# One recurrence-and-experts kernel: the token rows written in another order, by GpSimd's DMA queue in place of ScalarE's

## The chip, the cores and the metric

The kernel runs on one core of a Trainium2 chip. A core has TensorE (PE in the profile; its weight loads PEld), VectorE (DVE), ScalarE (ACT), GpSimd (POOL) and SyncE (SP), each with its own in-order instruction queue, and 16 DMA engines that all queues share. SP, ACT and POOL can start DMAs. A matrix product goes from SBUF to PSUM; what leaves PSUM is copied by VectorE or ScalarE.

The metric is the device time of one execution in microseconds. The kernel before takes 568.6 us, the median of three runs from 563.7 to 569.66.

## The reference

Two parts, one after the other. The first is a recurrence over 768 steps for 4 batches and 8 heads, with a state of 40 x 40 for each:

```python
for t in range(S):
    y[:, :, t] = np.einsum('bhd,bhde->bhe', rt, state)
    Sa = np.einsum('bhde,bhe->bhd', state, at)
    state_decay = state * wt[:, :, None, :] - np.einsum('bhd,bhe->bhde', Sa, bt)
    state = state_decay + np.einsum('bhd,bhe->bhde', vt, kt)
```

Its output y is turned into x, with 3072 rows (one a token, number batch * 768 + t) of 320 values. The second part picks one of 8 experts for each row, keeps for each expert the 80 rows with the largest gate value, and leaves all other rows of the output zero:

```python
expert_idx = np.argmax(x @ w_gate, axis=1)
tok_idx = ...            # the expert's rows, at most `capacity` of them, by gate_w
h = np.maximum(x[tok_idx] @ w1[e], 0.0)
out[tok_idx] = gate_w[tok_idx, None] * (h @ w2[e])
```

## The kernel before

**Tiling.** The sequence is cut into chunks of T = 64 steps (NCI = 12 chunks), and the batches into NP = 2 pairs. A unit is a chunk of a pair: 24 units, n = 2 * chunk + pair, and each fills 128 partitions with 2 batches x 64 steps. Four units make a batch of units (`batches`, six of them, kq = 0 to 5 in the code; the text says batch 0 to 5). For a chunk the recurrence is a triangular system. `prepare` makes decays and score matrices of a unit, `finish` makes its output and the new state, `gate` the gate values of a group of units. Groups are the same as batches, but for the last four units, which form two groups of two.

**The triangular systems.** Batch 0 is inverted by products on PE (`doubling`). For batches 1 to 5 `invert` writes the 32 x 32 diagonal blocks to HBM (L657, SP), reads them back with one block to a partition (`fetch`, L661, POOL), and eliminates on POOL: 30 steps of a multiply (L677) and an add (L679), a mask, a memset, and a copy that turns the blocks (`flip`, L691). POOL then writes both forms to HBM (`put`, L697: `solved`, `flipped`). SP brings them back into the layout of the units: d<-flipped (L719), nt<-solved (L713), d<-solved (L706). `solve` builds the rest of the inverse from these with two products, the first at L737 and the second at L752; ACT copies between them (gt, L742).

**Rows and gates.** ACT copies a unit's x into `xg` (L992), which holds one group. VectorE makes the gates (L1020 to L1034), and puts the gate value in the row's last column (L1033). `ids_go` (L1039, POOL) multiplies the one-hot expert choice with two numbers for each token, the tile `tok`. `rows_go` (L1048) writes `xg` to `x_rows` in HBM, in the order batch * 768 + t, by one DMA of 160.5 KB for each batch parity and pair of units, on ACT's queue. Eight DMAs on ACT's queue (L1118) write zeros over the output, 480 KB each.

**What sets the order.** A planner (`Plan`) takes every step with an engine, a planned duration, a lag, a due time and what it reads and writes, and lists all steps in one order. The calls are made in that order, so each engine's queue holds its steps in the list's order. `add("ACT", ...)` names the engine for the plan alone; the call inside the step decides which queue gets the instruction. The list around the fifth group, with planned times, reads: ... 357.24 flip of batch 5 (POOL), 358.36 `xg` of group 4 (VectorE), 358.66 `rows_go` of group 4 (ACT), 359.39 and 360.39 the two puts of batch 5 (POOL), 361.39 `ids_go` of group 4 (POOL). The eight zero steps stand at planned times 67, 102, 136, 166, 197, 224, 255 and 280.

**The second part.** After the last gate VectorE finds each expert's limit, PE turns the one-hot places into row numbers, and VectorE makes from them idx_g (which rows of x_rows to gather, L1224) and idx_s (which rows of the output to write, L1233). POOL gathers 128 rows at a time (L1155); six passes through the experts' two layers follow, and POOL scatters the results (L1303).

Of the kernel before, what the change touches and what calls it, by code (L numbers as in the profile page):

```python
# [8 lines left out]
F32 = mybir.dt.float32  # L9
# [4 lines left out]
Alu = mybir.AluOpType  # L14
# [3 lines left out]
class Plan:  # L18
# [7 lines left out]
    def add(self, eng, us, lag, when, fn, reads=(), writes=(), psum=None, to=()):  # L26
        whole = eng == "PE" and psum[0][0] in WHOLE
        o = dict(eng=eng, us=us, lag=lag, when=when, stage=self.stage, fn=fn, whole=whole, i=len(self.ops), deps=set(), psum=None,
                 reads=list(reads), writes=list(writes), to=list(to))
        if psum:  # L30
            key, n = psum
            if key not in self.width:
                self.width[key] = n
                o["psum"] = key
            o["writes"].append(key)
        o["kind"] = f"{eng} {(psum[0] if psum else [*o['writes'], *o['reads'], ('none', 0)][0])[0]}"
        for key in o["reads"]:
            for p, wrote in self.touch.get(key, ()):
                if wrote:
                    o["deps"].add(p)  # L40
        for key in o["writes"]:
            for p, _ in self.touch.get(key, ()):
                o["deps"].add(p)
        for key in o["reads"]:
            self.touch.setdefault(key, []).append((o["i"], False))
        for key in o["writes"]:
            self.touch.setdefault(key, []).append((o["i"], True))
        self.ops.append(o)
# [140 lines left out]
def kernel(  # L189
# [19 lines left out]
    nc = tc.nc  # L209
    B, H, S, D = r.shape  # L210
    N, DM = out.shape
    E = moe_w_gate.shape[1]
    F = moe_w1.shape[2]
    cap = min(int(moe_capacity), N)
    T, C, HB = 64, 32, 64
    NCI = S // T
    NP = B // 2
# [85 lines left out]
    with ExitStack() as p1:  # L303
# [88 lines left out]
        def iotas():  # L392
            nc.gpsimd.iota(first_i, pattern=[[-1, E]], base=E, channel_multiplier=0)
            for bb in range(2):
                nc.gpsimd.iota(tok_i[T * bb : T * bb + T, 0:NCI], pattern=[[1, NCI], [2 * NCI, NP]],
                               base=1 + NCI * bb, channel_multiplier=0)
                nc.gpsimd.iota(tok_i[T * bb : T * bb + T, NCI], pattern=[[0, NP]], base=0, channel_multiplier=1)

        add("POOL", 1.5, 0.1, -600.0, iotas, (), [("iotas", 0)])
# [601 lines left out]
        def gate(gi):  # L1001
# [40 lines left out]
            add("POOL", 0.8, 0.1, z + 1, ids_go, [sm, ("gates", gi), ("late", 0)], [("ids", gi), *([("og", gi)] if nu == GU else [])])  # L1042

            def rows_go():
                dst = x_dram[:, :].rearrange("(p b c t) d -> b t c p d", p=NP, b=2, t=T)
                for bb in range(2):
                    for i in range(nu // NP):
                        nc.scalar.dma_start(dst[bb, :, ns[0] // NP + i],  # L1048
                                          xg[T * bb : T * bb + T, NP * i : NP * i + NP, :])
            add("ACT", 0.65 * nu, 2.0, z + 2, rows_go, [("xg", gi)], ())  # L1050

            def ranks(src, dst, keys, us, wide):
# [62 lines left out]
                [("early", e), ("nt", NM + e), *((k_, NM + 2 * e + i) for i in range(2) for k_ in SLOT)])  # L1115
        zrows = 384
        for i in range(N // zrows):
            add("ACT", 0.7, 2.0, 0.0, lambda i=i: nc.scalar.dma_start(  # L1118
                out[i * zrows : (i + 1) * zrows, :].rearrange("(p r) (h d) -> p (r h) d", p=128, h=2),
                zero.to_broadcast([128, zrows // 64, DM // 2])), [("W", 2 * i)])  # L1120

# [31 lines left out]
    def gather(p):  # L1153
        rows[p] = fs.tile([128, XW], F32, name="rows", tag="rows", bufs=NPASS)
        nc.gpsimd.indirect_dma_start(  # L1155
            out=rows[p][:, 0:XW], out_offset=None, in_=x_dram[:, :],
            in_offset=bass.IndirectOffsetOnAxis(ap=of_pass(idx_g, p), axis=0))
# [6 lines left out]
    with ExitStack() as p2:  # L1164
        sl = p2.enter_context(tc.tile_pool(name="sl", bufs=1))
        ps_l = p2.enter_context(tc.tile_pool(name="ps_l", bufs=1, space=PSUM))
        NSEL = E * 2 * NM
        at = sl.tile([128, NM, 2 * E], F32, name="at")
        idle = ps_l.tile([128, NSEL], F32, name="idle")

        def keep_warm(n):
            for _ in range(n):
                nc.tensor.matmul(idle, lhsT=ident, rhs=at.rearrange("p m a -> p (m a)"), start=True, stop=True)

        thr = sl.tile([E, 1], F32, name="thr")
        nc.vector.tensor_scalar_max(thr, best[:, cap - 1 : cap], 1e-6)
        thw = sl.tile([E, 128], F32, name="thw")
        nc.vector.tensor_copy(thw, thr.to_broadcast([E, 128]))
        thp = ps_l.tile([128, E], F32, name="thr_p")
        nc.tensor.transpose(thp, thw, ident[:E, :E])  # L1180
        tb = sl.tile([128, E, 1], F32, name="tb")
        nc.vector.tensor_copy(tb[:, :, 0], thp)
        sel = sl.tile([128, E, 2, NM], BF16, name="sel")
        for i, op in enumerate((Alu.is_gt, Alu.is_equal)):
            nc.vector.tensor_tensor(out=sel[:, :, i, :], in0=gates.rearrange("p m e -> p e m"),
                                    in1=tb.to_broadcast([128, E, NM]), op=op)
        selm = sel.rearrange("p e i m -> p (e i m)")
        pos = ps_l.tile([128, NSEL], F32, name="pos")
        nc.tensor.matmul(pos, lhsT=less_b, rhs=selm, start=True, stop=False)
        upto = sl.tile([128, NSEL], BF16, name="upto")  # L1190
        nc.vector.tensor_tensor_scan(upto, seg.rearrange("p e m -> p (e m)"), selm, 0.0, op0=Alu.mult, op1=Alu.add)
        nc.tensor.matmul(pos, lhsT=ones_b, rhs=upto, start=False, stop=True)
        nc.vector.scalar_tensor_tensor(out=at.rearrange("p m a -> p a m"), in0=pos.rearrange("p (a m) -> p a m", m=NM), scalar=1.0,
                                       in1=sel.rearrange("p e i m -> p (e i) m"), op0=Alu.add, op1=Alu.mult)
        slot = sl.tile([128, NM, 1], F32, name="slot")
        nc.vector.tensor_reduce(slot[:, :, 0], at, axis=AX, op=Alu.add)
        keep_warm(1)
        ip = ps_l.tile([HW, 2 * E], F32, name="ids_p")
        CH = 8
        for m0 in range(0, NM, CH):  # L1200
            hot = sl.tile([128, CH, HW], BF16, name=f"hot{m0}")
            nc.vector.tensor_tensor(out=hot, in0=slot[:, m0 : m0 + CH].to_broadcast([128, CH, HW]),
                                    in1=iot.to_broadcast([128, CH, HW]), op=Alu.is_equal)
            for m in range(m0, m0 + CH):
                nc.tensor.matmul(ip, lhsT=hot[:, m - m0, :], rhs=ids[:, m].rearrange("p i e -> p (i e)"),
                                 start=m == 0, stop=m == NM - 1)
        i0 = sl.tile([HW, 2 * E], F32, name="i0")
        nc.vector.tensor_copy(i0, ip)
        spread = ps_l.tile([128, 2, 2, E], F32, name="spread")
        for i, n in enumerate((HB, C)):  # L1210
            for j in range(128 // n):
                nc.tensor.matmul(spread[n * j : n * j + n, i].rearrange("p i e -> p (i e)"),
                                 lhsT=ident[0:HW, HB * i : HB * i + n], rhs=i0, start=True, stop=True, skip_group_check=True)
        keep_warm(6)
        i1 = sl.tile([128, 2, 2, E], F32, name="i1")
        nc.vector.tensor_copy(i1, spread)
        num = sl.tile([128, 2, E], F32, name="num")
        nc.vector.scalar_tensor_tensor(out=num, in0=i1[:, :, 0, :], scalar=float(T), in1=i1[:, :, 1, :], op0=Alu.mult, op1=Alu.add)
        none = sl.tile([128, 2, E], F32, name="none")
        for i, n in enumerate((HB, C)):  # L1220
            per = 128 // n
            for j in range(per):
                part = slice(n * j, n * j + n)
                nc.vector.tensor_scalar(idx_g[i][part, 0 : E // per], num[part, i, j::per], -float(T), 0.0, op0=Alu.add, op1=Alu.max)  # L1224
            for p in range(NPASS):
                if column[p][0] == i and p < AHEAD:
                    gather(p)
        nc.vector.tensor_scalar(none, i1[:, :, 0, :], 0.0, float(4 * N), op0=Alu.is_equal, op1=Alu.mult)
        for i, n in enumerate((HB, C)):
            per = 128 // n  # L1230
            for j in range(per):
                part = slice(n * j, n * j + n)
                nc.vector.scalar_tensor_tensor(out=idx_s[i][part, 0 : E // per], in0=num[part, i, j::per], scalar=-float(T),  # L1233
                                               in1=none[part, i, j::per], op0=Alu.add, op1=Alu.add)

    for p in range(AHEAD, NPASS):
# [110 lines left out]
```

## Time and profile before

| | |
|---|---|
| median of three runs | 568.6 us (563.7 to 569.66) |
| profiled execution | 569.61 us, span of the instructions 567.5 us |
| PE busy | 454.1 us, 80% |
| VectorE busy | 339.3 us, 60% |
| ScalarE busy | 208.8 us, 37% |
| GpSimd busy | 222.8 us, 39% |
| granted TensorE clock, mean | 0.921 |
| DMA on SP's queue | 218360 packets, 51.15 MB |
| DMA on ACT's queue | 18176 packets, 9.19 MB |
| DMA on POOL's queue | 2736 packets, 9.67 MB |
| rows of x, ACT's queue | 24 DMAs of 160.5 KB, median 3.5 us to landing |
| zeros, ACT's queue | 8 DMAs of 480.0 KB, median 3.4 us to landing |

The profile is one execution. Busy times leave out instructions that issue DMAs on SP and ACT, and waits; the issuing of a DMA on POOL is listed with POOL's work. An arrow in a line (`<-`) names what ended the idle time before it. "SPq" and "ACTq" are the sequencers of SP and ACT, where DMAs are issued.

### The profile page before, as it was taken

Reading aid. Unit: us, or ns where it says so; the run is one execution under the profiler, and the core shown is the slowest. Engines: PE = TensorE matmul, PEld = TensorE weight load, DVE = VectorE, ACT = ScalarE, POOL = GpSimd, SP = SyncE. Lnnn points to the kernel's source line nnn. Section 1 sums busy time; section 2 is a strip of 40 time slices with the busy share of each in tenths; the row PEclk is TensorE's granted clock in tenths of the full one; section 3 lists DMA queues with packets and bytes.
Section 4 is the critical chain, followed back from the end, with each engine's and each line's share of the span. In section 5 each row is a group of like instructions: output and inputs, shape, how many; then the busy total and the mean of one; then the engine's idle time right before and its main releaser. Section 6 shows DMA issues by size and latency. Waiting matters only on the chain. (4 is left out here: it accounts for less than half of the span.)

```text
span 567.5 us, 28199 instructions
## 1 busy us (share of the span) xinstructions
PE 454.1 (80%) x12677; PEld 371.6 (65%) x12677; DVE 339.3 (60%) x752; ACT 208.8 (37%) x424; POOL 222.8 (39%) x412
## 2 busy tenths in 40 slices
PE   2868888689889998699985999399829860799996
PEld 2767777678778887588874988388828750434442
DVE  6879777265363895487663786374377688621211
ACT  1445465346533454245542455234314320021010
POOL 7000001895408982598404986388400000120101
PEclk9999999889987999789997899779968995599999
DMA  7645658433595658856687544832591539289600
GB/s 132 115 73 86 102 102 137 80 75 76 110 176 107 118 94 182 175 98 120 153 146 142 90 92 110 167 53 46 131 188 40 186 100 331 73 241 351 235 13 17
DMA packets 239392, 71.81 MB, mean 127 GB/s; under 512 B 216520, under 2 KB 233928, under 8 KB 239272
## 3 DMA queue, kind: packets, MB, share of 16 engines
q1 hardware_dynamic: 218360, 51.15, 45.5%
q10 hardware_dynamic: 18176, 9.19, 6.3%
q0 software_dynamic: 2736, 9.67, 5.1%
q8 instruction: 99, 1.62, 1.1%
q14 instruction: 21, 0.17, 0.1%
HBM read 52.11 MB, written 16.72 MB: 121 GB/s over the span
## 5 line engine op out<-in xcount | busy, mean ns | idle before, releaser
L677 POOL TENSOR_TENSOR tmp<-lt 128x30 f32<-128x30 f32 (+9 forms) x150 | 80.2, 534 | 34.5 <-DMA lt<-blocks 23.4
L679 POOL TENSOR_TENSOR lt<-lt,tmp 128x30 f32<-128x30 f32 (+9 forms) x150 | 86.6, 577 | 11.7
L661 POOL DMA_DIRECT2D lt<-blocks x5 | 2.9, 586 | 129.9 <-PE ps L437 79.9
L604 PE MATMUL ps<-slot,kbT 40*64 40x64 f32 x1536 | 34.7, 224 | 8.4 <-issue 4.9
L604 PEld LDWEIGHTS ps<-slot,kbT 40*64 40x64 f32 x1536 | 29.0, 136 | 12.1 <-issue 6.3
L543 DVE TENSOR_TENSOR_SCAN slot<-dec,begins 128x520 f32<-128x520 f32 x24 | 31.6, 1317 | 4.6 <-POOL cand L345 3.4
L930 PE MATMUL ps<-UL,slot 64*64 64x128 f32 x768 | 30.0, 293 | 2.3 <-DVE UL L818 1.9
L930 PE MATMUL ps<-VL,slot 64*64 64x128 f32 x768 | 27.8, 272 | 4.8 <-issue 4.7
L818 DVE TENSOR_TENSOR UL<-ps,mask 128x512 f32<-128x512 f32 x24 | 16.5, 688 | 24.8 <-PE ps L811 24.7
L551 DVE TENSOR_TENSOR_SCAN iv<-dec,ends 128x520 f32<-128x520 f32 x24 | 30.9, 1286 | 0.7
L973 DVE TENSOR_TENSOR xT<-ps,slot 128x512 f32<-128x512 f32 x24 | 16.5, 688 | 22.9 <-PE ps L930 22.9
L783 ACT COPY VL<-rawv 128x320 f32<-128x320 f32 x24 | 11.0, 459 | 50.3 <-PE ps L930 41.4
L437 PE MATMUL ps<-ident,slot 128*128 128x128 f32 x192 | 28.6, 297 | 0.9 <-issue 0.8
L593 ACT COPY kbT<-ps 128x1024 f32<-128x1024 f32 x24 | 24.4, 1015 | 13.3 <-PE ps L437 12.2
L1303 POOL DMA_INDIRECT out_dram<-y,idx_s x6 | 6.0, 994 | 57.3 <-DVE y L1302 57.3
L794 ACT COPY rv<-ps 128x1024 f32<-128x1024 f32 x24 | 24.3, 1013 | 10.7 <-PE ps L437 10.7
L1039 POOL TENSOR_TENSOR ids<-gsm,tok 128x32 bf16<-128x32 f32 (+1 forms) x14 | 3.0, 231 | 63.9 <-DVE gsm L1029 43.3
L624 DVE TENSOR_TENSOR slot<-ps,mask 128x512 f32<-128x512 f32 x24 | 16.4, 685 | 17.5 <-PE ps L604 17.5
L930 PEld LDWEIGHTS ps<-VL,slot 64*64 64x64 f32 x768 | 22.3, 135 | 6.8 <-issue 6.8
L985 PE MATMUL ps<-wsel,xT 128*128 128x88 f32 x192 | 25.8, 277 | 1.1 <-DVE xT L973 1.0
L930 PEld LDWEIGHTS ps<-UL,slot 64*64 64x64 f32 x768 | 23.3, 143 | 4.8 <-DVE UL L818 2.7
L985 PEld LDWEIGHTS ps<-wsel,xT 128*128 128x128 f32 x192 | 23.3, 191 | 2.5 <-DVE xT L973 1.5
(216 smaller groups left out, 1143.8 us busy)
## 6 DMA issues: line engine op xcount, KB each, us to landing
w<-in_moe_w_dram SPq DMA_DIRECT2D x4, 1280.0 KB
slot<-in_moe_w_dram SPq DMA_DIRECT2D x4, 1120.0 KB, 7.8
slot<-in_moe_w_dram SPq DMA_DIRECT2D x4, 1024.0 KB, 8.3
w<-in_moe_w_dram SPq DMA_DIRECT2D x4, 1024.0 KB, 11.9
x_rows<-xg ACTq DMA_DIRECT2D x24, 160.5 KB, 3.5
rawk<-in_k_dram SPq DMA_DIRECT2D x48, 80.0 KB, 3.0
raww<-in_w_dram SPq DMA_DIRECT2D x48, 80.0 KB, 3.1
rawr<-in_r_dram SPq DMA_DIRECT2D x48, 80.0 KB, 3.0
```

Of the source, the lines that this page charges most:

```text
L437: nc.tensor.matmul(o, lhsT=i, rhs=ident, start=True, stop=True, is_transpose=True, skip_group_check=True)
L543: nc.vector.tensor_tensor_scan(at("P", n), at("dec", n)[:, 0 : H * SEG], begins, 0.0, op0=Alu.mult, op1=Alu.add)
L551: nc.vector.tensor_tensor_scan(at("iv", n)[:, H * SEG : 0 : -1], at("dec", n)[:, H * SEG : 0 : -1], at("ends", n)[:, H * SEG : 0 : -1], 0. ...
L593: nc.scalar.copy(at("kbT", n).rearrange("p (k c) -> p k c", k=2), ps[:, bank(kk) : bank(kk) + 2, :])
L604: nc.tensor.matmul(ps[T * o : T * o + T, b0 + q, T * i : T * i + T], lhsT=at("kbT", n)[rows, 512 * x + c : 512 * x + c + T], rhs=at("ah", ...
L677: e.tensor_tensor(out=tv, in0=t3[:, 0:s, s : s + 1].to_broadcast([np_, s, n]), in1=t3[:, s : s + 1, s + 1 :].to_broadcast([np_, s, n]), op ...
L679: e.tensor_tensor(out=t3[:, 0:s, s + 1 :], in0=t3[:, 0:s, s + 1 :], in1=tv, op=Alu.add)
L794: nc.scalar.copy(at("rv", n).rearrange("p (k c) -> p k c", k=2), ps[:, bank(kr) : bank(kr) + 2, :])
L818: nc.vector.tensor_tensor(out=view(at(name, n), 512, (HB, 2), (2 * HB, 4), (1, T)), in0=view(ps[:, bank(key), :], 0, (512, 2), (T, 4), (1, ...
L930: nc.tensor.matmul(ps[HB * q : HB * q + HB, b0 + bb, 128 * i : 128 * i + 128], lhsT=at("kb", n)[rows, o : o + HB], rhs=view(at(name, n)[ro ...
L973: nc.vector.tensor_tensor(out=view(at("xT", n), 0, (T, 2), (128, M4), (1, T)), in0=view(ps[:, bank(ky), :], HB, (512, 2), (128, M4), (1, T ...
L985: nc.tensor.matmul(ps[:, b0, o : o + 88], lhsT=at("xT", n)[:, 128 * i : 128 * i + 128], rhs=wsel[:, i, :], start=True, stop=True, skip_gro ...
```

## The change

Each group's rows are written by one DMA on POOL's queue, in the order of the units: row 128 * n + p for partition p of unit n. The zeros of the output are issued on POOL's queue as well. The numbers in `tok` follow the new order (`iotas`), so that 64 * number + step gives a row of x_rows. The gather uses this directly (`put`). The scatter needs the token's place in the output; five VectorE operations make it from the same numbers, by rounding to find the chunk. The planner's entries are as they were.

```diff
-                nc.gpsimd.iota(tok_i[T * bb : T * bb + T, 0:NCI], pattern=[[1, NCI], [2 * NCI, NP]],
-                               base=1 + NCI * bb, channel_multiplier=0)
+                nc.gpsimd.iota(tok_i[T * bb : T * bb + T, 0:NCI], pattern=[[2 * NP, NCI], [2, NP]], base=1 + bb, channel_multiplier=0)
...
             def rows_go():
-                dst = x_dram[:, :].rearrange("(p b c t) d -> b t c p d", p=NP, b=2, t=T)
-                for bb in range(2):
-                    for i in range(nu // NP):
-                        nc.scalar.dma_start(dst[bb, :, ns[0] // NP + i],
-                                          xg[T * bb : T * bb + T, NP * i : NP * i + NP, :])
+                dst = x_dram[128 * ns[0] : 128 * ns[-1] + 128, :].rearrange("(u p) d -> p u d", p=128)
+                nc.gpsimd.dma_start(dst, xg)
             add("ACT", 0.65 * nu, 2.0, z + 2, rows_go, [("xg", gi)], ())
...
-            add("ACT", 0.7, 2.0, 0.0, lambda i=i: nc.scalar.dma_start(
+            add("ACT", 0.7, 2.0, 0.0, lambda i=i: nc.gpsimd.dma_start(
                 out[i * zrows : (i + 1) * zrows, :].rearrange("(p r) (h d) -> p (r h) d", p=128, h=2),
                 zero.to_broadcast([128, zrows // 64, DM // 2])), [("W", 2 * i)])
...
-        num = sl.tile([128, 2, E], F32, name="num")
-        nc.vector.scalar_tensor_tensor(out=num, in0=i1[:, :, 0, :], scalar=float(T), in1=i1[:, :, 1, :], op0=Alu.mult, op1=Alu.add)
+        num, put = (sl.tile([128, 2, E], F32, name=n) for n in ("num", "put"))
+        nc.vector.scalar_tensor_tensor(out=put, in0=i1[:, :, 0, :], scalar=float(T), in1=i1[:, :, 1, :], op0=Alu.mult, op1=Alu.add)
...
-                nc.vector.tensor_scalar(idx_g[i][part, 0 : E // per], num[part, i, j::per], -float(T), 0.0, op0=Alu.add, op1=Alu.max)
+                nc.vector.tensor_scalar(idx_g[i][part, 0 : E // per], put[part, i, j::per], -float(T), 0.0, op0=Alu.add, op1=Alu.max)
...
+        chunk, ROUND = sl.tile([128, 2, E], F32, name="chunk"), 1.5 * 2**23
+        nc.vector.tensor_scalar(chunk, i1[:, :, 0, :], 1.0 / B, -(B + 1) / (2.0 * B), op0=Alu.mult, op1=Alu.add)
+        nc.vector.tensor_scalar_add(chunk, chunk, ROUND)
+        nc.vector.tensor_scalar(chunk, chunk, -ROUND, float(T - B * S), op0=Alu.add, op1=Alu.mult)
+        nc.vector.scalar_tensor_tensor(out=num, in0=i1[:, :, 0, :], scalar=float(S), in1=i1[:, :, 1, :], op0=Alu.mult, op1=Alu.add)
+        nc.vector.tensor_tensor(out=num, in0=num, in1=chunk, op=Alu.add)
...
-                nc.vector.scalar_tensor_tensor(out=idx_s[i][part, 0 : E // per], in0=num[part, i, j::per], scalar=-float(T),
+                nc.vector.scalar_tensor_tensor(out=idx_s[i][part, 0 : E // per], in0=num[part, i, j::per], scalar=-float(S),
                                                in1=none[part, i, j::per], op0=Alu.add, op1=Alu.add)
```

## The prediction

> **What bounds the kernel now.** I read the page's slices first, then the waits, then SP's own waits, then the timeline around the places they point at.
>
> The slices (here of 14.2 us) show TensorE (PE) busy all the way, with dips that recur: each digit is tenths of a slice, and PE falls at slices 29 to 32 while POOL is busy or idle in blocks.
>
> ```profile
> PE   2868888689889998699985999399829860799996
> ...
> POOL 7000001895408982598404986388400000120101
> ```
>
> POOL's blocks are the five eliminations (L677, L679), one for each batch of four units after the first. The waits say what PE's dips end on. Columns: who waited on whom, us in all, times, longest.
>
> ```profile
> PE ps L737 <- DMA d<-flipped: 18.9, 3, 9.7
> ...
> PE ps L737 <- DMA d<-solved: 8.2, 1, 8.2
> ...
> PE ps L604 <- ACT gt L742: 1.8, 1, 1.8
> ```
>
> L737 is the first product of a batch. It needs what POOL's elimination gave, carried by POOL's two puts (L697) to HBM and by SP's transfers back (L706, L713, L719). By stretches of the same view these waits are 3.3 us at batch 2 (ending 235.4), 5.9 at batch 3 (303.1), 9.7 at batch 4 (369.6), 8.2 at batch 5 (423.4): 27 us in which PE does nothing. The rest of the main part is PE at its own pace. So the change is worth what it does to these four waits. SP's own waits show who else takes part in them:
>
> ```profile
> SPq L430 <- DMA x_rows<-xg: 12.6, 8, 6.3
> ...
> SPq L706 <- DMA out_dram<-zero: 5.9, 2, 4.1
> SPq L719 <- DMA x_rows<-xg: 5.7, 1, 5.7
> ```
>
> SP waits for the landing of ACT's transfers, though it reads nothing of theirs. The trace's operands say why: SP's and ACT's DMAs take turns at eight completion semaphores, and a DMA waits for the last user of its number. POOL's DMAs have eight numbers of their own. At batch 4 SP stood from 359.74 to 365.49 for a semaphore that a row transfer of ACT (issued 362.34) raised at 365.48; the flipped put had landed at 355.53. At batch 2 d<-solved stood until 234.79 for a zero transfer that landed at 234.78.
>
> The timeline at batch 5 has what the change turns round. Columns: start, us, engine, line, operation.
>
> ```profile
> 401.09 1.98 POOL L691 COPY ltT<-lt 128x1024 f32<-128x1024 f32 x1
> ...
> 403.37 0.58 POOL L697 DMA_DIRECT2D flipped<-ltT  x1 [0.30 <-POOL ltT L691]
> ...
> 403.95 0.55 POOL L697 DMA_DIRECT2D solved<-lt  x1
> ...
> 414.52 0.17 DVE L1033 COPY xg<-gsm 128x4 f32<-128x4 f32 x1
> 414.56 2.83 SPq L719 DMA_DIRECT2D d<-flipped  x2
> ...
> 414.72 2.87 ACTq L1048 DMA_DIRECT2D x_rows<-xg  x4
> ...
> 417.49 1.76 SPq L713 DMA_DIRECT2D nt<-solved  x2
> ...
> 423.42 1.12 PE L737 MATMUL ps<-d,nt 128*64 128x64 f32 x16 [8.16 <-DMA d<-solved]
> ```
>
> **Order after the change.** The planner still plans both steps as ACT work, so the list that it writes is the same list; only the engine that gets the call differs. In that list the row step of group 0 to 3 stands beside POOL's ids of that group (L1039), the zeros stand in or between eliminations, and the row step of group 4 stands between the flip (L691) and the two puts of batch 5.
>
> **ACT's queue.** Gone are 24 row issues of 624 ns (15.0 us) and 8 zero issues of 574 ns (4.6 us). Most of it lay where ACT had nothing due. On the path: after the issues of 307.19 ACT's gt came 3.6 us late and PE stood 1.8; about 0.5 at 236.66. I take -2 (bounds -4 and 0).
>
> Here the Trainium skill speaks against a larger gain: "DMA: Bandwidth & Descriptors", under "Issuing engines are not separate DMA queues", says that starting DMAs on another engine saves only the issuing sequencer's time, since the same 16 engines carry them. By it the sum would end at -2. The SP rows above say that issue order also costs landings of other queues, so I go on by the rows.
>
> **SP's queue.** Batch 2: d<-solved leaves up to 4.1 us earlier; PE lost 3.3 and then 1.6 there. The zero still follows the fetch, now in POOL's queue, so the first loss mostly stays: -2 (-4 to 0). Batch 3: ACT's zero of 293.49 (768 packets of 640 B at 32 ns, over 16 engines 1.6 us) ran just before d<-flipped; SP's issues stretched to 1.6 and 2.2 us, POOL's fetch waited to 295.97. In the new order this zero follows the fetch, behind SP's transfers: -3 (-5 to +1). Batch 4: SP is free 5.7 us earlier, but lt<-blocks (packets until 364) and the rows of group 3 now flow from POOL's queue in just that time; in the records SP's 128 B packets nearly stop while such a transfer runs (from over 1000 in a us to 60 to 160). So most of the 5.7 turns into a wait for the DMA engines: -1 (-5.7 to +1). Raw loads (12.6 us of waiting): PE waits for none of them after the first 60 us: 0 (-1 to 0).
>
> **POOL's queue.** A transfer of 128 descriptors of 4096 B costs POOL 532 to 582 ns, an indirect one of 128 costs 956 to 982. The new ones have 512 (rows) and 768 (zeros). Bounds: flat, 0.53; in proportion to 532, 2.1 and 3.2. The indirect row tells of dearer descriptors too, but of index reading; I take 1.4 and 2.0, a little below the middle of flat and proportional for rows, at it for zeros. Seven row steps and eight zeros are about 25 us of POOL, laid beside covers: zero 1 beside the 13.1 us wait of the first flip; zero 2 beside 8.8 us idle before fetch 2; zeros 4 and 6 and row step 3 beside the 4.5 to 6.6 us landing of a fetch. A zero and a row step (3.4 together, at most 5.3) lengthen eliminations 2, 3 and 4. Their puts landed 6.7, 12 and 4.2 us before SP turned to the flipped ones: covered but at batch 4, where the earlier main chain takes 3 to 5 us of cover: +0.5 (0 to +4); without any cover each would cost its 3.4.
>
> The other page against it is "SBUF — State Buffer", "SBUF: two separate sides": descriptor writing on GpSimd is locked out while VectorE runs some two-port operations; it gives a DMA of 620 ns that took 3100. The nearest rows: one fetch of 0.80 in place of 0.53, and eliminations' operations of 1.4 to 1.5 in place of 0.65. By rows it is under 1 us a time; by the page 2.5 each on the rows and two puts of batch 5, +7.5. I take the rows; the rest is in the range.
>
> **Batch 5.** POOL's row step of group 4 waits for xg, complete at 414.69, and the puts queue behind it: they leave at about 416.1 and 416.7 in place of 403.37 and 403.95. SP, PE and, through PE, everything later wait for these puts. Rows' data (3072 packets of 76 ns over 16 engines and six equal groups: 2.4 us) goes first on the same queue, from about 1.5 us after the issue; then flipped (128 packets of 170 ns: 1.4 us) and solved. That makes flipped land 6.5 us after the row step starts and solved 7.9. SP's d<-flipped then goes at 421.3 in place of 414.56. Back come its own issues: without ACT's beside them 0.6 each in place of 1.4 (2.4 us for both pairs), and no row data beside nt<-solved. From 414.6: solved at 7.9, nt<-solved issued by 9.2, packets to 11.3, landing 12: L737 at about 427.2 in place of 423.4. +4.3 with 0.5 for the semaphore turn (bounds: +2 when the puts' data are quick, +10 when all of the lateness in the puts stays: 12.7 later, less the 5.8 for which flipped had lain ready, plus generation and rows' data).
>
> **Small things.** Zero 0 now goes at about 12 us, beside the first loads, which PE waits for: 1.6 us of transfer, +0.3 (0 to +1.6). Five more VectorE operations of 0.17 plus a gap of 0.04 make 1.05 us before idx_s; the gather's landing leaves VectorE 3.6 us idle there, so 0 (without it +1.05). `put` is the old `num`, so gathers leave as before. Iotas: 0.
>
> **Sum.** -2 -2 -3 -1 +0.5 +4.3 +0.3 = -2.9, against the profiled execution's 569.6 (span 567.5 and 2.1 around it): 566.7. The median of the three runs is 568.6, 1 below that execution: 565.5.
>
> **Rivals.**
> - *Relief whole* (chance 0.24). SP's transfers of batches 3 and 4 slip in before POOL's fetch and rows, so that batch 4's 5.7 and batch 3's 5 come in full: -6 more, 559.5. For it: the stop at 359.74 has no other reason. Against: fetch and rows in the same 5 us.
> - *The held puts* (0.20), slower. Place: POOL between the flip and the puts of batch 5. Price: up to +10 as above, in place of 4.3, and batch 4's +4, as generation is proportional; with 3 of the relief gone too, 565.5 + 5.7 + 3.5 + 3 = 577.7. It decides from a lateness of L737 above 7.5, the sum of the gains. For it: the wait is certain, only its slack is not.
> - *Nothing that counts* (0.10). The DMA engines are the limit in these stretches (DMA share 0.86 to 1.14 in the four waits I looked at), so order moves little and the loss is small too: 568 to 570.
> - *My forecast* (0.46): 565.5, own range 560 to 571.
>
> **Numbers.** About 1% (5.7 us) is what a measurement of this kernel can tell from no change. Faster than 562.9: all of the first rival, 0.13 of the forecast: 0.37. Slower than 574.3: the second rival: 0.20. Between: 0.43. Range 555 to 577: below it and above it lie about 0.1 each.
>
> **What would show it.** After: no wait of SP on x_rows or zeros; no row or zero issue on ACT's queue; PE's waits at the first product shorter in batches 2 and 3, about as long in batch 4, longer by some 4 in batch 5; a POOL wait on VectorE's xg copy of some 11 us before the batch 5 puts; row issues of 1 to 2 us on POOL. The forecast is wrong if POOL's issues cost more than 3 us, if the puts of batch 5 land later than 8 us after the row step, or if batch 4's wait falls by more than 3.

## The result, and the profile after

The changed kernel takes 573.58 us (median of 6 runs, 572.56 to 575.78), the kernel before 567.68 on the same chip (6 runs, 563.70 to 569.66): a ratio of 1.0145, 95% interval 1.0109 to 1.0181. It is slower by about 1.5%. A second set of runs of the changed kernel on another chip gave 1.0143 (1.0059 to 1.0227). The profiled execution has a span of 574.0 us, the one before 567.5. The ratios here and below leave out executions more than 1.5% above the fastest of their kernel; where a kernel scatters more widely than that, the median of all its runs is given beside.

The prediction was 565.5 (own range 560 to 571), with a gain of 2.9 us; the loss is 5.9 us by these medians and 8.2 by the ratio, taken of 568. First the row of PE and the row of POOL in the slices (14.35 us each here):

```profile
PE   2868888698879999599968997499639760899995
...
POOL 8000004882418981599617983588300000210101
```

PE's dips are about where they were, and the slices are too coarse to show what has moved. The waits of PE over the whole span (who waited on whom, us in all, times, longest):

```profile
PE ps L736 <- DMA d<-flipped: 15.2, 3, 7.5
...
PE ps L736 <- DMA nt<-solved: 9.2, 1, 9.2
...
PE ps L1059 <- POOL og L1040: 3.8, 1, 3.8
```

L736 (before: L737) is the first product of a batch. In sum its waits are 24.4 us, before 27.1, but they have moved: 18.9 for the flipped blocks in three batches became 15.2, and batch 5's 8.2 became 9.2, with another 3.8 just ahead of it, where PE's transposition of the gates (L1059) waits for a POOL copy. In the kernel before that line reads:

```profile
PE ps L1063 <- POOL og L1041: 1.0, 1, 1.0
```

Taken together PE now stands 13.0 us there (3.8 + 9.2), before 9.2 (1.0 + 8.2): +3.8.

SP's own waits hold no row and no zero any more. Most of what is left stands ahead of its loads of raw inputs (L429):

```profile
SPq L429 <- PE ps L436: 39.2, 15, 8.9
SPq L429 <- ACT VL L782: 30.6, 9, 5.6
SPq L429 <- ACT uT L899: 26.8, 3, 14.3
...
SPq L718 <- DMA flipped<-ltT: 4.8, 1, 4.8
```

The last line is new: SP waits for the flipped put of batch 5 itself, which before had long landed. The timeline at batch 5 shows why (start, us, engine, line, operation, in brackets the idle time before it and what ended it):

```profile
402.08 2.00 POOL L690 COPY ltT<-lt 128x1024 f32<-128x1024 f32 x1
...
413.24 0.16 DVE L1032 COPY xg<-gsm 128x4 f32<-128x4 f32 x1
...
413.96 0.82 POOL L1045 DMA_DIRECT2D x_rows<-xg  x1 [9.88 <-DVE xg L1032]
414.78 0.55 POOL L696 DMA_DIRECT2D flipped<-ltT  x1
415.32 0.55 POOL L696 DMA_DIRECT2D solved<-lt  x1
...
420.08 1.01 SPq L718 DMA_DIRECT2D d<-flipped  x2
421.30 1.00 SPq L712 DMA_DIRECT2D nt<-solved  x2
422.34 2.27 SPq L705 DMA_DIRECT2D d<-solved  x4
```

The flipped blocks lie ready at 404.1, and POOL stands 9.9 us for VectorE's gates of group 4, because the row step is ahead of the puts in its queue. The puts leave at 414.78 and 415.32 in place of 403.37 and 403.95, and SP's transfers back start at 420.08 in place of 414.56. The stretch from the first product of batch 4 to that of batch 5 shows the price, and one that comes with it. Busy us of PE, its weight loads, VectorE, ScalarE and POOL, then the granted clock, the DMA share and GB/s; first the kernel before, then the changed one:

```profile
369.60:423.40 53.80, 41.41 (x1362) 37.56 (x1363) 31.88 (x94) 19.42 (x45) 31.28 (x57) 0.88 0.50 103
```

```profile
365.70:426.20 60.50, 44.24 (x1364) 40.24 (x1365) 32.87 (x97) 19.34 (x45) 36.13 (x68) 0.81 0.46 97
```

The stretch is 6.7 us longer. PE's pauses are some 4 of it; 2.8 are PE's own busy time, at a granted clock of 0.81 in place of 0.88.

### The profile page after: what moved, and what is told of

The parts are those of the page before. It is cut to its first block, busy times and chain, and to the rows that moved or that the text cites. A ratio compares the mean times of both kernels' runs of the same rounds, so it can differ in the third digit from the quotient of the medians.

```text
span 574.0 us, 28192 instructions
## 1 busy us (share of the span) xinstructions
PE 461.5 (80%) x12677; PEld 378.5 (66%) x12677; DVE 338.4 (59%) x757; ACT 208.9 (36%) x424; POOL 237.0 (41%) x427
## 3 DMA queue, kind: packets, MB, share of 16 engines
q0 software_dynamic: 4640, 17.55, 9.2%
q10 hardware_dynamic: 8448, 1.31, 1.4%
HBM read 52.11 MB, written 16.72 MB: 120 GB/s over the span
## 5 line engine op out<-in xcount | busy, mean ns | idle before, releaser
L676 POOL TENSOR_TENSOR tmp<-lt 128x30 f32<-128x30 f32 (+9 forms) x150 | 81.7, 544 | 31.0 <-DMA lt<-blocks 20.2
L603 PE MATMUL ps<-slot,kbT 40*64 40x64 f32 x1536 | 35.2, 228 | 7.1 <-issue 5.7
L603 PEld LDWEIGHTS ps<-slot,kbT 40*64 40x64 f32 x1536 | 29.5, 139 | 10.4 <-issue 6.6
L817 DVE TENSOR_TENSOR UL<-ps,mask 128x512 f32<-128x512 f32 x24 | 16.5, 688 | 27.6 <-PE ps L810 27.4
L592 ACT COPY kbT<-ps 128x1024 f32<-128x1024 f32 x24 | 24.4, 1015 | 14.3 <-PE ps L436 12.0
L817 DVE TENSOR_TENSOR VL<-ps,mask 128x512 f32<-128x512 f32 x24 | 16.5, 687 | 15.9 <-PE ps L810 14.3
```

What stands on the lines that cost most here:

```text
L592: nc.scalar.copy(at("kbT", n).rearrange("p (k c) -> p k c", k=2), ps[:, bank(kk) : bank(kk) + 2, :])
L603: nc.tensor.matmul(ps[T * o : T * o + T, b0 + q, T * i : T * i + T], lhsT=at("kbT", n)[rows, 512 * x + c : 512 * x + c + T], rhs=at("ah", ...
L676: e.tensor_tensor(out=tv, in0=t3[:, 0:s, s : s + 1].to_broadcast([np_, s, n]), in1=t3[:, s : s + 1, s + 1 :].to_broadcast([np_, s, n]), op ...
L817: nc.vector.tensor_tensor(out=view(at(name, n), 512, (HB, 2), (2 * HB, 4), (1, T)), in0=view(ps[:, bank(key), :], 0, (512, 2), (T, 4), (1, ...
```

## The experiments

The theory that the experiments test: the loss is the wait of the two puts for VectorE, and the relief of 8 us on which the prediction set its sum isn't there. Its rival: the loss is the new traffic in GpSimd's queue and the added operations, and the puts' lateness is covered.

Each result below gives the median of all runs of that kernel, then the ratio to the kernel before on the same chip with its 95% interval, and the us that this ratio makes of 568.

**The hold alone.** The kernel before, with one small POOL copy that reads group 4's gate column where the row step stands:

```diff
             def rows_go():
+                if gi == 4:
+                    nc.gpsimd.tensor_copy(held, xg[:, :, DM])
```

> The kernel before, with one GpSimd copy of group 4's gate column (128x4) put between the flip and the two puts of batch 5, so that the puts wait for VectorE as in the changed kernel; rows and zeros stay with ScalarE. Held-puts theory: no relief, the full loss: 572 to 576 us, with the puts leaving near 415 and a longer PE wait at the first product of batch 5 (12 us or more). Rival theory (the lateness is covered, the loss is in the traffic and the added operations): 566 to 569 us, as before.

Measured: 573.47 us, 1.0117 (1.0055 to 1.0178), +6.6 us. No row, no zero and no VectorE operation was changed. Its timeline at batch 5, POOL alone:

```profile
412.30 0.19 POOL L1047 COPY held<-xg 128x4 f32<-128x4 f32 x1 [12.54 <-DVE xg L1034]
412.53 0.58 POOL L698 DMA_DIRECT2D flipped<-ltT  x1
413.11 0.55 POOL L698 DMA_DIRECT2D solved<-lt  x1
```

and two of PE's waits there, from the waits between 140 and 440 us:

```profile
PE ps L738 <- DMA nt<-solved: 10.1, 1, 10.1
...
PE ps L1066 <- POOL og L1042: 2.9, 1, 2.9
```

A 0.19 us copy costs what the whole change costs, as far as the intervals tell. That the hold alone is sufficient is shown.

**The hold taken away.** The changed kernel with group 4's row step behind the two puts:

```diff
         listed = plan.order()
+        at_row = (index of the fifth rows_go in listed)
+        at_put = (index of the last of POOL's two puts of batch 5)
+        listed.insert(at_put, listed.pop(at_row))
```

> The changed kernel, but group 4's row step goes to GpSimd's queue behind the two puts of batch 5 and not ahead of them. Held-puts theory (the loss is the wait of these two puts for VectorE's gates): the puts leave near 404 again, PE's wait at the first product of batch 5 falls from 9.2 us by about 4, and what the lateness dragged along (the slow clock after the pause) falls with it: 565 to 569 us, at or below the kernel before. Rival theory (the loss comes from the new traffic itself, rows and zeros in GpSimd's queue and on the DMA engines, and from five more VectorE operations at the end; the puts' lateness is covered as it was): 572 to 574 us, as the changed kernel.

Measured: 570.60 us, 1.0068 (1.0024 to 1.0113), +3.9 us. That lies between the two forecasts: roughly half of the loss goes, but the kernel isn't back at or below the one before. Something else in the change costs, or at any rate the reliefs don't show. PE's idle time in the 16 us ahead of batch 5's first product, added up from the trace, tells the hold from everything else without an exception:

| kernel | us idle | hold |
|---|---|---|
| changed; changed, second chip | 14.1; 13.9 | yes |
| hold alone | 14.0 | yes |
| changed, zeros on ScalarE | 13.6 | yes |
| before | 11.0 | no |
| before, zeros on POOL | 11.0 | no |
| changed, puts first | 10.6 | no |
| new order alone | 10.2 | no |
| changed, puts first, zeros on ScalarE | 10.0 | no |

The means are 13.9 and 10.6: the hold costs 3.3 us at this place, where kernels of one kind lie within 0.5 us with the hold and 1.0 without. Over the whole run the hold alone cost more, 6.6 us.

**Where the parts stand alone.** Zeros back on ScalarE's queue (`nc.gpsimd.dma_start` to `nc.scalar.dma_start` in the zeros' line), all else as changed:

> The changed kernel with the eight zero transfers back on ScalarE's queue; rows as changed. Held-puts theory: the zeros hardly matter, 571 to 575 us; part of the gain at batch 3 (3 us) goes, since it was put down to the zero that ran just before the flipped transfer. Rival theory (zeros lengthen the eliminations and fill GpSimd's queue): 568 to 570 us.

Measured: 1.0071 (1.0014 to 1.0127); its 12 runs scatter from 567 to 580 with a median of 575.69. By the median it is where the changed kernel is, by the ratio some 4 us below. It doesn't decide between the two; the opposite edit does. The kernel before with the zeros alone on POOL's queue:

> The kernel before with only the eight zero transfers moved to GpSimd's queue. By the prediction: about -3 for batch 3, +0.5 for longer eliminations, +0.3 for the first loads, so 565 to 567 us. If zeros in GpSimd's queue cost (as the changed kernel with the puts first, still 3 us above before, lets one suspect): 570 to 573 us. If they do nothing: 567 to 569 us.

Measured: 567.15 us, 0.9993 (0.9942 to 1.0045). The zeros in POOL's queue neither gain nor cost, to within some 3 us.

The new order of rows alone, with one row transfer per group on ScalarE's queue and the zeros there too (both `nc.gpsimd.dma_start` of the change to `nc.scalar.dma_start`):

> Only the new order of rows and the coalescing: one row transfer per group on ScalarE's queue, zeros on ScalarE's queue, GpSimd's queue as before the change. The later row numbers (five VectorE operations) and all else as changed. Held-puts theory: no held puts and half of ScalarE's issues gone, 565 to 568.5 us, at or a little below the kernel before. Rival theory (the new row order, its bigger packets and the five operations cost by themselves): 570 to 574 us.

Measured: 568.84 us, 1.0028 (0.9983 to 1.0074). ScalarE's row issues fell from 24 of 624 ns to 7 of 375, so 12 us of its queue are gone, and the kernel is no faster. SP's waits on the landings of ScalarE's transfers are in this kernel:

```profile
SPq L705 <- DMA out_dram<-zero: 8.3, 3, 4.7
SPq L705 <- DMA x_rows<-xg: 7.4, 1, 7.4
SPq L429 <- DMA x_rows<-xg: 6.5, 2, 4.8
SPq L300 <- DMA x_rows<-xg: 5.2, 1, 5.2
```

That is 27.4 us of such waits, where the kernel before has 24.2, and the two kernels take the same time.

The rows on POOL with no hold, zeros on ScalarE (the two edits above together):

> The changed kernel with both suspects taken back: zeros on ScalarE's queue, and group 4's row step behind the puts of batch 5; rows otherwise by one transfer per group on GpSimd's queue. If the reliefs are real and only the held puts (and the zeros' queueing) ate them: 561 to 565 us. If the reliefs are nothing and the held puts are all: 567 to 570 us, as before the change.

Measured: 569.74 us, 1.0053 (1.0001 to 1.0104). No wait of SP on a row is left in it, and it is no faster than the new order alone, nor than the kernel before. The changed kernel with the puts first has neither a row nor a zero among SP's waits, and was 3.9 us slower than the kernel before. So removing the waits that the prediction set out to remove doesn't shorten the run; the gain of some 8 us that it counted for them and for ScalarE is refuted.

The changed kernel itself, beside these:

> The changed kernel itself, beside the others on their chip: 572 to 576 us by its first runs. The held-puts theory wants it level with the kernel that has the wait alone (573.5 us there).

Measured: 574.16 us, 1.0143 (1.0059 to 1.0227).

**Is there anything to relieve?** The kernel before without any row or zero transfer (the gathers then read a weight tensor, so that x_rows isn't needed):

```diff
-                        nc.scalar.dma_start(dst[bb, :, ns[0] // NP + i],
-                                          xg[T * bb : T * bb + T, NP * i : NP * i + NP, :])
...
-            add("ACT", 0.7, 2.0, 0.0, lambda i=i: nc.scalar.dma_start(
+            add("ACT", 0.7, 2.0, 0.0, lambda i=i: i < 0 and nc.scalar.dma_start(
...
-            out=rows[p][:, 0:XW], out_offset=None, in_=x_dram[:, :],
+            out=rows[p][:, 0:XW], out_offset=None, in_=(N x XW rows of moe_w1),
```

> The kernel before without any of the row and zero transfers (the part of the computation left out: x_rows and the zeros of the output are not written; the gathers read as many rows of a weight tensor instead). It is the most that relief of ScalarE's and SP's queues could ever bring. The prediction's sum of reliefs (2 for ScalarE, 2, 3 and 1 for the waits of batches 2 to 4): 559 to 561 us, 8 below the kernel before or more. Rival theory (these waits end on other things as soon as the first one is gone, so there was nothing to win): 565 to 569 us.

Measured: 558.59 us, 0.9848 (0.9796 to 0.9900), -8.6 us. So the writes do cost what the prediction hoped to get back. In the trace the three stretches from the first product of batch 1 to that of batch 4 take 190.6 us; in the nine traces of the table above 196.8 to 201.9. It isn't the gathers that gain by no longer reading x_rows: from batch 5's first product to the end this kernel takes 147.1 us, the one before 144.1.

The same with all 32 issues kept, each of 64 numbers from one row:

```diff
-                        nc.scalar.dma_start(dst[bb, :, ns[0] // NP + i],
-                                          xg[T * bb : T * bb + T, NP * i : NP * i + NP, :])
+                        nc.scalar.dma_start(dst[bb, :, ns[0] // NP + i][0:1, 0:1, 0:64],
+                                          xg[T * bb : T * bb + 1, NP * i : NP * i + 1, 0:64])
```

(and the zeros likewise, 64 numbers of one row of `out`).

> The kernel before with all its 32 row and zero issues on ScalarE's queue, but each writes only 64 numbers of one row (the part left out: nearly all of x_rows and of the output's zeros; the gathers read rows of a weight tensor). Issues and turns at the semaphores stay, the bytes go. If the 9 us that the writes cost are their traffic on the DMA engines: 558 to 561 us, as without any writes. If they are ScalarE's issue time (15 + 5 us on its queue) and SP's waits for its turn: 565 to 568 us.

Measured: 560.72 us, 0.9865 (0.9819 to 0.9911), -7.7 us. The queues of the three kernels (packets, MB, share of 16 engines; q10 carries ScalarE's transfers); before, without the bytes, and changed, where q0 is POOL's:

```profile
q10 hardware_dynamic: 18176, 9.19, 6.3%
```

```profile
q10 hardware_dynamic: 8512, 1.32, 1.4%
```

```profile
q0 software_dynamic: 4640, 17.55, 9.2%
```

The 64 packets by which the second exceeds q10 of the changed kernel (8448) are all that is left of rows and zeros, with their 32 issues, and the gain stays. So it is the 7.9 MB that cost; whether at the DMA engines or in HBM these runs don't tell. Two reserves: an issue of 64 numbers took ScalarE 256 ns in place of 624, so this kernel relieves its queue too, and SP's waits on rows and zeros fell with the bytes, from 24.2 us to 8.6. But the new order alone relieved ScalarE by as much, the changed kernel with the puts first has no such wait of SP, and neither gained. The change carries the same 7.9 MB on another queue: q0 went from 9.67 MB to 17.55, and "written" is 16.72 MB in both.

**Whose bytes.** Without the zeros, and without the rows:

> The kernel before without the eight zero transfers (left out: the zeros of the output), rows as before. It splits the 9 us by which the kernel without any of these writes is shorter. In proportion to packets' time (zeros 8 x 1.6 = 13 us of the engines, rows 6 x 2.4 = 14.6): about half, 563 to 564 us. If only rows cost: 567 to 569 us. If only zeros: 558 to 560 us.

Measured: 566.12 us, 1.0010 (0.9964 to 1.0056): nothing by the ratio, -3.1 us by the medians of all runs.

> The kernel before without the 24 row transfers (left out: the writing of x_rows; the gathers read rows of a weight tensor), zeros as before. If rows are what costs: 560 to 562 us, 7 below before (without zeros it was 1.3 below, without both 9). If rows and zeros share the cost or only their sum is too much: 564 to 567 us.

Measured: 563.89 us, 0.9937 (0.9891 to 0.9982), -3.6 us by the ratio and -6.6 by the medians of all runs, since that set of the kernel before ran up to 582.8. By either measure rows are the larger part; whether both together save more than the sum of each stays open.

**A place where the bytes don't hurt?** Some 5 us after a batch's first product the DMA engines are nearly idle (in the kernel before share 0.02 from 375 to 380 us, after the first product of batch 4 at 369.6). Two kernels moved the steps of groups 0 to 4, with two zeros each, to just ahead of the next group's first copy into xg (L991): one from ScalarE's queue, one from POOL's with group 4's on ScalarE's:

```diff
+        for g in range(5):
+            late = [rows_ops[g], *zero_ops[2 * g : 2 * g + 2]]
+            listed = [x for x in listed if not any(x is y for y in late)]
+            at_copy = (index of x_copy of unit 4 * (g + 1) in listed)
+            listed[at_copy:at_copy] = late
```

> The new order of rows, one transfer per group on ScalarE's queue, but each group's row step and two zeros with it moved back in the list to just ahead of the next group's first copy into xg, when the batch's fetch from HBM is over and the DMA engines are nearly idle. If the writes cost because they run beside the transfers that a batch's first product waits for: 560 to 564 us. If their traffic costs wherever it runs: 567 to 570 us.

> The changed kernel with the row steps of groups 0 to 3 and two zeros with each moved back in the same way, on GpSimd's queue, inside an elimination; group 4's row step goes to ScalarE's queue after the first products of batch 5, so nothing holds the puts. By the theory of the window: 560 to 564 us. If GpSimd's time in the eliminations is what counts (three issues of 0.8 us each): 567 to 571 us.

Measured: 579.94 us, 1.0263 (1.0193 to 1.0334), and 572.80 us, 1.0069 (1.0024 to 1.0114). Both miss, by a fault of the experiment: xg has one buffer. ScalarE in the second, at batch 5:

```profile
432.59 0.40 ACTq L1045 DMA_DIRECT2D x_rows<-xg  x1
439.91 0.42 ACT L991 COPY xg<-ps 128x320 f32<-128x320 f32 x1 [6.32 <-DMA x_rows<-xg]
```

The copy waits until the row transfer ahead of it has been read out, 6.3 us here and 15 in all. So the steps were moved again: groups 0 to 3 some 6 us of the list earlier than that, group 4 after the second product of batch 5 (on ScalarE's queue) in one kernel, and right behind the puts in the other, which leaves the zeros where they were before the change:

> The changed kernel, but row steps of groups 0 to 3 stand some 6 us of the list ahead of the next group's first copy into xg (several elimination steps later on GpSimd's queue, past the fetch window, early enough that the copy does not wait), two zeros each just ahead of that copy, and group 4's row step on ScalarE's queue after the second product of batch 5. Theory of the window (rows cost by running beside the transfers that the first product waits for): 561 to 565 us. Theory of the amount: 567 to 570 us. Either way no held puts.

> The same for the row steps of groups 0 to 3; group 4's goes on GpSimd's queue right behind the two puts of batch 5, zeros stay on ScalarE's queue at their old places. Theory of the window: 562 to 566 us (batch 5's fetch still has the rows of group 4 beside it). Theory of the amount: 567 to 570 us.

Measured: 569.53 us, 1.0004 (0.9941 to 1.0067), and 569.58 us, 1.0053 (1.0005 to 1.0102). In the first no copy waits for a row transfer any more (SP does once, for 1.8 us, in the second part), and it only comes level with the kernel before. By the whole time the theory that the bytes cost because of where they run isn't borne out. By the parts, each read from one execution, it may be half right. From the first product of batch 1 to that of batch 5 the first of these kernels takes 249.0 us; the one before takes 255.8, the changed one 258.4 and 258.8, the one without the writes 242.9. But its first product of batch 1 comes 3.2 us later than in the kernel before, and what follows the first product of batch 5 takes 147.5 us in place of 144.1, so nothing is left of it. Why these two parts are longer stays open.

Most of what the bytes cost shows at the transfers back. PE's waits at L737 and L752 between the first products of batches 1 and 5 add up to 31.7 us before, to 29.1 and 29.0 in the two executions of the changed kernel, and to 20.0 without the writes and 19.4 without their bytes. With the rows moved (group 4's on ScalarE's queue) they are 25.1, which is within the 23.6 to 30.3 of the other kernels that move all bytes. Of the kernels that compute the whole result none is faster than the kernel before beyond its uncertainty.

## Why the prediction was wrong, step by step

**Batch 5 (+4.3)** was right. Row step ahead of the puts, POOL waiting for VectorE, L736 at 426.16 (forecast 427.2). The batches before came 3.8 us earlier in this execution than in the one before, so the fair measure starts at the end of VectorE's gates: from there to L736 it is 12.8 us (forecast 12.5, before 8.7). PE's extra pause is thus 4.0 by this distance and 3.3 by the table. SP turned to the flipped blocks 6.1 us after the row step began (forecast of their landing: 6.5). Over the whole run the hold costs more than that pause: +6.6 alone (3.1 to 10.1). A part of the excess may be the clock: the profiles show the half-speed clock for 22.9 and 21.1 us between the first products of batches 4 and 5 of the changed kernel, for 12.9 before; but the new order alone, without the hold, had 21.6, so this isn't shown.

**ScalarE's queue (-2), batches 2 and 3 (-2, -3)** is where it failed. The prediction put it so: "The SP rows above say that issue order also costs landings of other queues, so I go on by the rows." The rows were read rightly, as waits that end on ScalarE's transfers; what doesn't follow is that without them SP's transfers land earlier by as much. The runs: 12 us less on ScalarE's queue gained nothing (1.0028); the zeros on POOL gained nothing (0.9993); no SP wait on a row gained nothing (1.0053), and none on a zero either gained nothing (1.0068); only taking the bytes away did (0.9865). The rule that the prediction weighed against the rows, in the Trainium skill's "DMA: Bandwidth & Descriptors", under "Issuing engines are not separate DMA queues", is the one that these runs bear out: the same engines carry the bytes whoever starts them. Even the 2 us of ScalarE's issue time didn't show in the run, though the one wait of PE that they were read from did shrink (for gt at L604, 1.8 us before; at L603, 0.2 after).

PE's waits at the first products of batches 2, 3 and 4 of the changed kernel:

```profile
235.59 1.12 PE L736 MATMUL ps<-d,spare_nt 128*64 128x64 f32 x16 [4.84 <-DMA d<-flipped]
...
299.99 1.12 PE L736 MATMUL ps<-d,nt 128*64 128x64 f32 x16 [2.86 <-DMA d<-flipped]
...
365.74 1.12 PE L736 MATMUL ps<-d,spare_nt 128*64 128x64 f32 x16 [7.49 <-DMA d<-flipped]
```

Batch 2's wait, forecast to shrink by 2 us, grew from 3.3 to 4.8 (5.0 in the second trace). With these 7 us at zero the prediction's own sum is -1 +0.5 +4.3 +0.3 = +4.1, on the side of the 5.9 to 8.2 measured; the 1.8 to 4.1 us that are missing are about what the hold costs above its pause (6.6 less 3.3).

**Batch 3's -3 looked right, and was not.** The changed trace shows the stretch from batch 2's to batch 3's first product 64.4 us long, the one before 67.6. But with the hold alone, where rows and zeros stand on ScalarE as before, it is 64.6 too (and PE's wait 3.5 us, in place of 5.9 before), and in the second trace of the changed kernel 66.4. One execution's 3 us in one stretch was within what executions of like kernels differ by, and the gain that seems to answer the forecast comes from a single execution, as the forecast did.

**Batch 4 (-1)** was right in its reasoning. SP's transfers back, first before, then after:

```profile
365.55 1.02 SPq L719 DMA_DIRECT2D d<-flipped  x2
366.67 2.31 SPq L706 DMA_DIRECT2D d<-solved  x4
```

```profile
358.21 2.43 SPq L718 DMA_DIRECT2D d<-flipped  x2
360.73 4.75 SPq L705 DMA_DIRECT2D d<-solved  x4
```

SP starts 7.3 us earlier, but its six issues take 7.3 us in place of 3.4, and the first product comes 7.5 us after the start in place of 4.0. The same shows in the second trace (7.9) and with rows on POOL and no hold (7.9), against 4.4 with the hold alone. The time that the semaphore had taken goes to the busy DMA engines (share 1.08 from 358 to 366 us of the changed kernel). The same reasoning, carried over to batches 2 and 3, might have taken most of their gain away.

**POOL's issue price** was too high: a row step took POOL 0.76 to 0.84 us (taken: 1.4), a zero 0.80 to 1.04 (taken: 2.0). Of the bounds, 0.53 flat and 2.1 or 3.2 in proportion, the flat one was near. The lock-out of descriptor writing, for which the prediction estimated up to +7.5 us, isn't seen: none of these 15 issues took longer than 1.04 us. The rival of the held puts had the direction right, but its size (577.7) needed proportional prices; the loss came with the forecast's own +4.3 at batch 5 and without the reliefs.

**The five VectorE operations (0)** can't be told from nothing. From the first gather to the end the kernels with the new order of rows take 74.5 to 75.9 us, those with the old 74.1 to 75.3.

What remains after the hold, 1 to 3 us of loss with rows on POOL (1.0053, and 1.0068 with the zeros there too, against 1.0028 with the new order alone), lies within the intervals' overlap and has no cause shown.

Three small slips of the prediction change nothing in this: 568.6 less 2.9 is 565.7, not 565.5; the 24 row issues of the kernel before take 17.1 us together, not 15.0, since some are longer than their median of 624 ns; and PE's row of slices dips in single slices (the 22nd, 26th and 30th, at 5, 3 and 2), not from 29 to 32.

## What to carry to other kernels

A wait that ends on another transfer's landing names who was last, not who is guilty: before counting it as a gain, ask whether the transfers behind it would find the DMA engines free, and test it by taking the bytes away and keeping the issue. Before a DMA moves to another engine's queue, look at what stands behind it there: here a step whose data came 10 us late held two transfers that were ready and that the next stage waited for. And a stall of a few us read from one execution should be seen in a second one before it enters a sum.

## What the runs showed of the hardware that had not been expected

- The price of starting a transfer from GpSimd's queue is nearly flat: 0.53 to 0.63 us for 128 pieces of 4096 B (one of 0.80), 0.76 and 0.78 for 256 of 1284 B, 0.77 to 0.84 for 512 of them, 0.80 to 1.04 for 768 of 640 B.
- On ScalarE's queue one transfer of a whole group took 375 ns to start, less than one of the four that it replaces (624 ns); a transfer of 64 numbers took 256.
- Executions of one kernel on one chip spread over 562 to 576 us (the kernel before, 29 runs), and the first product of batch 1 alone stood between 164.8 and 172.1 us in the traces of kernels that differ little until then.
